# Attention and an MLP on one core: the first batch's value path, the planner's prices and search, and two tiles

## The chip, the cores and the metric

One core of a Trainium2 chip runs the kernel. The time is that of the device in microseconds, the median of several executions; lower is better. The matmul engine is called TensorE (PE in the rows; PEld is its loading of weights), VectorE is DVE, ScalarE is ACT, GpSimd is POOL, and SyncE is SP. SP issues every DMA of this kernel, from one queue, in order.

## The reference

Four batches, 8 heads, 576 positions, head size 64. After the rotation of q and k come softmax attention, a low-rank mixing over the positions, and an MLP with a rectifier; all in float32.

```
q, k = rotate(q), rotate(k)                    # [4, 8, 576, 64]
attn = softmax(q @ k.T / 8)
x    = (attn @ v) as [4, 576, 512]
h    = x.T @ U @ V                             # U [576, 32], V [32, 576]
u    = x + h.T
out  = u + relu(u @ w_ch1) @ w_ch2             # w_ch1 [512, 2048], w_ch2 [2048, 512]
```

U, V and the two weight matrices arrive as 8-byte floats.

## The kernel before

Attention works on pairs of heads (`hp`, four to a batch) and on tiles of 128 query rows (`t`, five to a pair, the last with 64 rows). An ordinary tile has one score tile of 128 x 576 for each of the two heads; the last one holds the 64 rows of both heads in one. That makes nine score tiles a pair. `softmax_tile` takes the row maximum on VectorE (into a scrap tile, `unread`), the exponential on ScalarE, and hands the probabilities to the value matmuls in one of two ways:

- The plain path (`plain_pv`, true for head pairs below `HV` in batch 0; `HV` is 2): five float32 transposes on TensorE by the identity, two copies out of PSUM on ScalarE into a `pt32` tile, and in `values` five float32 matmuls against the values as they are. The sum of the exponentials comes from ScalarE's accumulator.
- The float16 path (all others): ScalarE writes a float16 copy, GpSimd the remainder (`two(p16[:, S:2 * S], p, p16[:, 0:S], ALU.subtract, ...)`), SP issues one DMA transpose of both into a `pt` tile, and `values` runs 14 float16 matmuls against split values (`vh`, `vl`, `vb`). `load_v` makes these from the loaded values: squares on ScalarE for a scale, a high and a low part, and DMA copies. In batch 0 it does so only for the heads from `2 * HV` on, and loads the others straight into `v32`.

`mix` then multiplies by U and V, and `mlp` runs over half batches of 288 positions. The first half of batch 0 is plain as well (`PLH` is 1): float32 matmuls with the weights as `weight` leaves them. `weight` loads 512 KB pieces, 32 in all (16 for each matrix), into staging parts of the tile `wt`, later of `x` and `u`, and `single` turns 8-byte into 4-byte floats with three bit operations a piece on VectorE. When the first half has used them, `convert1` and `convert2` take the squares on ScalarE (scrap output `junk`, which is part of a tile that `unread` uses too), a scale, and then `weight_halves` for each group: ScalarE writes the high float16 half of group g, VectorE or GpSimd the low one. Group g's raw words lie in slot g + 1 of `wt`, so its halves overwrite the raw words of group g - 1. The later half batches run three float16 matmuls for each product, interleaved with the attention of the next batch.

The order on every engine is computed before the kernel is emitted. `Plan` collects each instruction or group as a node with what must come before it; `cost` prices it, `lag` the time between two engines, `place` finds the earliest gap on its engine (a DMA needs a gap on SP's queue, `HW`, and one on the DMA engines), and where several engines can do the work it takes the earliest end. `shares` says which instructions of VectorE and GpSimd exclude each other on a shared port, which is a resource of its own. `schedule` runs a forward pass, then six times a backward pass, whose late times give the next forward pass its order, and keeps the best:

```
best = self.forward(sorted(range(len(key)), key=lambda n: key[n]))
for i in range(6):
    late = self.backward()
    span = self.forward(sorted(late, key=lambda n: (late[n], n)))
    best = min(best, span, key=lambda x: x[0])
```

The nodes are emitted in the order of their planned starts, so every queue runs in this order. All rows carry line 312, where `emit` makes the calls; tiles are told apart by their names.

Of the kernel before, what the change touches and what calls it, by code (L numbers as in the profile page):

```python
# [5 lines left out]

# [5 lines left out]
F32 = mybir.dt.float32  # L12
F32R = mybir.dt.float32r
# [11 lines left out]

PLAIN = HV = 2
GB = 0
# [7 lines left out]
BES = 1  # L35
SKEW = 1

FB = 2


class Plan:
# [86 lines left out]
    def cost(calls):  # L128

        us = 0  # L130
        for eng, op, a, k in calls:
# [5 lines left out]
            if eng == "tensor":  # L137
                m = free(a[1] if op == "transpose" else a[2])
                if op == "transpose":
                    us += free(a[0]) / 1200  # L140
                elif a[2].dtype == F32:

                    k = 2 if list(a[1].ap)[0][1] <= 64 and m > 256 and len(calls) == 4 else 1
                    us += max(m * 4, 640 if free(a[1]) > 1 and m > 1 else 256) / 2400 / k
                    us += 0.05 * (k > 1)
                else:
                    k = 2 if list(a[1].ap)[0][1] <= 64 and len(calls) == 12 else 1
                    us += max(m, 64) * (4 if a[2].dtype == F32R and m < 256 else 1) / 2400 / k
# [9 lines left out]
            elif op == "memset":  # L158
                us += 0.035 + n * 0.00083
            elif op == "tensor_tensor":  # L160
                us += 0.148 + n * (0.0021 if k["in1"].dtype in (F32, F32R) else 0.00189)
            else:
                us += 0.161 + 0.083 * by + n * 0.00083
        return us

# [33 lines left out]

    def place(self, ways, before):  # L200

        found = []
        for calls in ways:
            eng, op, a, k = calls[0]
            ready = max(
                [self.end[j] + self.lag(self.eng[j], eng) for j in before],
                default=0.0,
            )
            if eng == "sync":
                out, in_ = k.get("out", a[0] if a else 0), k.get("in_", a[1] if a else 0)  # L210
                if op == "dma_start_transpose":
                    hw, d = 0.62, 1.01
                else:
                    sb = out if out.space != bass.MemoryType.DRAM else in_
                    rows = list(sb.ap)[0][1]
                    hw, d = 0.45 if rows == 128 else 0.62, rows * free(sb) * SIZE[sb.dtype] / 360e3

                t2 = ready + hw + 0.65
                while True:
                    t2 = self.gap("DMA", t2, d)  # L220
                    t = self.gap("HW", t2 - hw - 0.65, hw)
                    if t <= t2 - hw - 0.65 + 1e-6:
                        break
                    t2 = t + hw + 0.65
                end = t2 + d
                found.append((end, end, t, calls, [("HW", t, hw), ("DMA", t2, d)]))
            else:
                d = self.cost(calls)
                t = self.gap(eng, ready, d)
                held = [eng] + ["port"] * self.shares(calls)  # L230
                while len(held) > 1:
# [10 lines left out]
    @staticmethod  # L242
    def lag(a, b):

        if a == "sync":
            return 0.94
        if a == b:
# [3 lines left out]
    def schedule(self):  # L251
        key = [n[2] for n in self.nodes]
        for n in reversed(range(len(key))):
            for j in self.nodes[n][1]:
                key[j] = min(key[j], (*key[n][:2], j))
        self.key = key
        self.after = [[] for _ in self.nodes]
        for n, (_, before, _) in enumerate(self.nodes):
            for j in before:
                self.after[j].append(n)  # L260
        best = self.forward(sorted(range(len(key)), key=lambda n: key[n]))
        for i in range(6):
            late = self.backward()
            span = self.forward(sorted(late, key=lambda n: (late[n], n)))
            best = min(best, span, key=lambda x: x[0])
        _, self.start, self.end, self.eng, self.chosen, self.busy = best

    def forward(self, order):
# [3 lines left out]
        for n in order:  # L272
            ways, before, _ = self.nodes[n]
            self.end[n], self.start[n], self.chosen[n], held = self.place(ways, before)
            self.eng[n] = self.chosen[n][0][0]
# [5 lines left out]
    def backward(self):  # L281
# [3 lines left out]
        for n in sorted(self.start, key=lambda n: (-self.end[n], -n)):  # L285
            s, e = self.start[n], self.end[n]
            if self.eng[n] == "sync":
                (_, _, hw), (_, _, d) = self.held[n]
                e = s + hw + 0.65 + d
                held = [("HW", e - s - hw, hw), ("DMA", 0.0, d)]  # L290
            else:
                held = [(dev, 0.0, d) for dev, _, d in self.held[n]]
            t = max(
                [done[j] + self.lag(self.eng[n], self.eng[j]) for j in self.after[n]],
                default=0.0,
# [40 lines left out]
def tile_rope_attention_then_mixer(ctx, tc, qk, v, tab, u_in, v_in, w1, w2, out):  # L336
# [83 lines left out]

    wt = cst.tile([P, 2 * NG + 1, 4 * DM], F16, name="wt")
    vst = cst.tile([P, S], F32R, name="vst")
# [184 lines left out]
    def raw_of(g):  # L607
        return wt[:, g + 1, :].bitcast(F32)

# [4 lines left out]

    slot = [pieces(wt[:, s:s + 2, :].rearrange("p s k -> p (s k)")) for s in range(NG + 1, 2 * NG + 1, 2)]
    big = pieces(xs_[1].rearrange("p c s -> p (c s)")[:, NP * S - 4 * DM:] if 1 else xs_[1].rearrange("p c s -> p (c s)")[:, 0:4 * DM])
# [9 lines left out]
    junks = [cst.tile([P, S], BF16, name=f"junk{i}") for i in range(3)]  # L626
    junk = junks[0][:, 0:DM]

# [802 lines left out]
```

## Time and profile before

| | us |
|---|---|
| median of three runs | 686.9 |
| the runs | 682.67, 686.9, 691.01 |
| span of the profiled execution | 684.8 |
| TensorE busy in it | 638.9 |
| VectorE, ScalarE, GpSimd busy | 427.6, 388.4, 232.0 |
| DMA: bytes, share of 16 engines | 86.92 MB, 56% |

The profile is of one execution on the core; its span runs from its first to its last instruction, and its time outside the span was not taken. Busy times of engines overlap. Times in the rows are microseconds from the start of the span unless marked ns. The granted clock of TensorE is 1.00 at 2.4 GHz and 0.50 at 1.2 GHz.

### The profile page before, as it was taken

The numbers are of one execution on the slowest core, as the hardware profiler recorded it, in microseconds if no ns is written. First come the engines' busy times: TensorE is split into PE (matmuls) and PEld (weight loads), VectorE is DVE, ScalarE is ACT, GpSimd is POOL, SyncE is SP. The second block draws the span as 40 slices with busy tenths as digits, with TensorE's granted clock in tenths as the row PEclk, the third lists the DMA queues.
The fourth block names the chain that finished last, engine by engine and source line by source line (L and its number), as shares of the span: only waits on it lengthen the run. The fifth ranks groups of instructions, "written<-read, shape, count | busy, mean of one in ns | idle before, by whom it ended". The sixth has DMA issues, their size and how long they took to land.

```text
span 684.8 us, 15181 instructions
## 1 busy us (share of the span) xinstructions
PE 638.9 (93%) x5952; PEld 486.2 (71%) x5952; DVE 427.6 (62%) x1089; ACT 388.4 (57%) x840; POOL 232.0 (34%) x208
## 2 busy tenths in 40 slices
PE   2899778999898999999999999999999999999997
PEld 1677656677666677777677767777776777777776
DVE  4989687978865765467775875657758652430210
ACT  3756575359887778447765765468566762220210
POOL 1110363113345667154445554264445351000000
PEclk9999899999999999999999999999999999999999
DMA  7799997466464577435768558157664583000000
GB/s 237 243 305 309 246 191 128 155 171 184 93 132 97 123 125 149 92 93 140 158 129 132 119 114 154 64 148 170 118 122 79 88 114 62 18 1 27 10 11 26
DMA packets 178345, 86.92 MB, mean 127 GB/s; under 512 B 152033, under 2 KB 167521, under 8 KB 178273
## 3 DMA queue, kind: packets, MB, share of 16 engines
q1 hardware_dynamic: 178272, 85.96, 56.1%
q8 instruction: 46, 0.75, 0.4%
q14 instruction: 27, 0.21, 0.1%
HBM read 41.70 MB, written 4.72 MB: 68 GB/s over the span
## 4 chain that ended last, share of the span: by engine, by line
PE 57%; DMA 12%; DVE 11%; issue 7%; ACT 6%; POOL 6%; SPq 1%; POOLq 0%; ACTq 0%; DVEq 0%
PE mm L312 42%; PE s L312 10%; DMA pt<-p 9%; PE pv L312 5%; POOL p L312 3%; ACT p L312 3%; DVE wt L312 3%; DVE junk L312 2%; DVE raw L312 2%; DMA raw<-qk 2%; POOL raw L312 2%; DVE qk L312 1%; ACT wt L312 1%; ACT junk L312 1%; SPq L312 1%
## 5 line engine op out<-in xcount | busy, mean ns | idle before, releaser
L312 PEld LDWEIGHTS <-wt 128*128 128x128 f16 x2688 | 256.0, 98 | 73.9 <-issue 12.4
L312 POOL TENSOR_TENSOR p<-p,p 128x576 f16<-128x576 f32 x120 | 158.0, 1328 | 192.8 <-ACT p L312 141.3
L312 PE MATMUL mm<-room,wt 128*128 128x288 f16 (+1 forms) x1472 | 217.9, 298 | 0.0
L312 PE MATMUL mm<-u,wt 128*128 128x288 f16 x1344 | 180.2, 287 | 2.0 <-DVE room L312 2.0
L312 ACT ACTIVATE room<-mm 128x288 f16<-128x288 f32 (+3 forms) x139 | 56.1, 410 | 104.7 <-PE mm L312 104.4
L312 DVE SCALAR_TENSOR_TENSOR room<-mm,room 128x288 f16<-128x288 f32 x112 | 50.8, 456 | 69.1 <-ACT room L312 68.6
L312 PEld LDWEIGHTS <-pt 128*128 128x128 f16 x1722 | 68.4, 98 | 27.3 <-DMA pt<-p 19.7
L312 PE MATMUL s<-qk,qk 64*128 64x288 f16 (+1 forms) x640 | 75.2, 357 | 11.5 <-DVE qk L312 11.2
L312 ACT ACTIVATE p<-p 128x576 f16<-128x576 f32 x120 | 79.3, 681 | 5.2 <-DMA pt<-p 4.0
L312 DVE TENSOR_SCALAR_CACHE_REDUCE junk<-s,bqk 128x576 bf16<-128x576 f32 x72 | 58.0, 811 | 23.0 <-PE s L312 19.6
L312 ACT ACTIVATE p<-s,nb,bqk 128x576 f32<-128x576 f32 x72 | 59.4, 829 | 18.4 <-DVE nb L312 13.2
L312 DVE TENSOR_SCALAR_CACHE_REDUCE junk<-s 128x576 bf16<-128x576 f32 x72 | 52.2, 753 | 27.3 <-PE s L312 24.4
L312 PE MATMUL pv<-vh,pt 128*128 128x65 f16 (+2 forms) x600 | 57.9, 203 | 9.3 <-DMA pt<-p 8.8
L312 ACT ACTIVATE p<-s,nb 128x576 f32<-128x576 f32 x72 | 51.9, 737 | 19.4 <-DVE junk L312 18.2
L312 PE MATMUL pv<-vl,pt 128*128 128x64 f16 (+2 forms) x600 | 57.7, 202 | 0.0
L312 ACT ACTIVATE xf<-pv,rc 128x64 f32<-128x64 f32 (+1 forms) x108 | 29.0, 309 | 43.6 <-DVE rc L312 40.5
L312 PEld LDWEIGHTS s<-qk,qk 64*128 64x128 f32 x256 | 26.0, 203 | 19.4 <-DVE qk L312 11.2
L312 DVE SCALAR_TENSOR_TENSOR ob<-mm,so,x 128x288 f32<-128x288 f32 x28 | 14.4, 513 | 40.5 <-PE mm L312 40.4
L312 DVE TENSOR_SCALAR rs<-pv,sc_v 128x2 f32<-128x2 f32 x63 | 13.7, 218 | 38.8 <-PE pv L312 38.7
L312 PE MATMUL mm<-x,wt 128*128 128x288 f32 x128 | 34.7, 423 | 1.9 <-ACT xf L312 1.1
L312 PE MATMUL pv<-vb,pt 128*128 128x65 f16 (+1 forms) x448 | 33.3, 197 | 0.0
L312 DVE SCALAR_TENSOR_TENSOR wt<-wt 128x512 int32<-128x512 int32 x46 | 31.9, 728 | 0.1
(161 smaller groups left out, 754.9 us busy)
## 6 DMA issues: line engine op xcount, KB each, us to landing
raw<-qk SPq DMA_DIRECT2D x30, 576.0 KB, 4.2
wt<-w SPq DMA_DIRECT2D x23, 512.0 KB, 6.2
out_t<-ob SPq DMA_DIRECT2D x32, 144.0 KB, 1.8
x<-w SPq DMA_DIRECT2D x6, 512.0 KB, 4.5
raw<-vt SPq DMA_DIRECT2D x6, 512.0 KB, 4.2
pt<-p SPq DMA_TRANSPOSE x120, 3.4
vb<-vh SPq DMA_DIRECT2D x6, 264.0 KB, 3.5
u<-w SPq DMA_DIRECT2D x3, 512.0 KB, 4.8
```

The costliest lines, as they stand in the source:

```text
L312: getattr(getattr(nc, eng), op)(*a, **k)
```

## The change

Head pairs 0 and 1 of batch 0 take the float16 path too (`HV` is 0), so the whole first batch does, and `load_v` splits all heads. The raw words of group g move from slot g + 1 to slot g + 2 of `wt` (`RS`), which has one slot more. The scrap tile `junk` gets memory of its own (`SQJ`). The planner's prices change: DMA transposes cost 1.37 us on SP's queue and 1.3 us on the DMA engines (0.62 and 1.01 before), other DMAs signal later, and several matmul groups cost 0.05 to 0.3 us more. `schedule` first does what it did, then applies 52 moves one after the other: each adds seeded random shifts to the late times in one stretch, plans three times, and is kept if the planned end is earlier. The memory set aside for DMA descriptors made by GpSimd becomes 1024 bytes a partition.

```
-PLAIN = HV = 2
+PLAIN = HV = 0
...
+RS = 2
+MOVES = (
+    (2201, 0.3, -489, 100), (7090, 0.3, -200, 40), (3748, 0.3, -65, 10), (365, 0.3, -230, 10),
...
+)
+SQJ = 1
...
                 if op == "transpose":
                     us += free(a[0]) / 1200
+                    if "xf" in a[1].tensor.name:
+                        us += 0.05 if free(a[0]) > 64 else 0.12
...
+        if eng == "tensor" and op == "matmul":
+            if list(a[1].ap)[0][1] <= 64 and len(calls) in (4, 12):
+                us += 0.18 if len(calls) == 12 else 0.06
+            elif len(calls) == 5 and free(a[2]) == 256:
+                us += 0.3
+            elif a[2].dtype == F32R:
+                us += 0.07
+            elif free(a[2]) <= 2:
+                us += 0.12
...
+    @staticmethod
+    def transfer(calls):
+
+        _, op, a, k = calls[0]
+        out, in_ = k.get("out", a[0] if a else 0), k.get("in_", a[1] if a else 0)
+        if op == "dma_start_transpose":
+            return 1.37, 0.9, 1.3, 0.98
+        sb = out if out.space != bass.MemoryType.DRAM else in_
+        rows = list(sb.ap)[0][1]
+        hw = 0.45 if rows == 128 else 0.62
+        return hw, hw + 0.65, rows * free(sb) * SIZE[sb.dtype] / 360e3, 1.2
...
         if a == "sync":
-            return 0.94
+            return 0.98 if turn else 1.2
...
+        best = self.settle(sorted(range(len(key)), key=lambda n: key[n]), 7)
+        for seed, width, begin, wide in MOVES:
+            best = min(best, self.shaken(best, seed, width, begin, wide), key=lambda x: x[0])
...
+    def shaken(self, best, seed, width, begin, wide):
+
+        draw = Random(seed)
+        late = {
+            n: t + draw.gauss(0, width) if begin <= t < begin + wide else t
+            for n, t in sorted(best[-1].items())
+        }
+        for n in reversed(range(len(late))):
+            for j in self.nodes[n][1]:
+                late[j] = min(late[j], late[n])
+        return self.settle(sorted(late, key=lambda n: (late[n], n)), 3)
...
-    wt = cst.tile([P, 2 * NG + 1, 4 * DM], F16, name="wt")
+    wt = cst.tile([P, 2 * NG + RS, 4 * DM], F16, name="wt")
...
-        return wt[:, g + 1, :].bitcast(F32)
+        return wt[:, g + RS, :].bitcast(F32)
...
-    junk = junks[0][:, 0:DM]
+    junk = cst.tile([P, DM], BF16, name="junk") if SQJ else junks[0][:, 0:DM]
...
-    nc = bacc.Bacc("TRN2", target_bir_lowering=False, num_devices=1)
+    nc = bacc.Bacc(
+        "TRN2", target_bir_lowering=False, num_devices=1,
+        dynamic_dma_scratch_size=1024,
+    )
```

## Rows read from the trace of the kernel before

**Rows 1.** the page: busy time by engine; shares of the chain that ended last

```profile
...
PE 638.9 (93%) x5952; PEld 486.2 (71%) x5952; DVE 427.6 (62%) x1089; ACT 388.4 (57%) x840; POOL 232.0 (34%) x208
...
PE 57%; DMA 12%; DVE 11%; issue 7%; ACT 6%; POOL 6%; SPq 1%; POOLq 0%; ACTq 0%; DVEq 0%
...
```

**Rows 2.** stages: busy us (x instructions) by engine, granted clock, DMA share, GB/s

```profile
...
0.00:13.00 13.00, 1.75 (x8) 1.18 (x8) 5.43 (x15) 4.36 (x7) 1.66 (x12) 1.00 0.71 220
13.00:74.00 61.00, 56.32 (x372) 44.37 (x368) 55.73 (x137) 39.73 (x116) 6.82 (x10) 0.97 0.89 288
43.00:69.00 26.00, 25.32 (x180) 20.25 (x181) 25.35 (x63) 17.06 (x50) 0.79 (x1) 1.00 0.92 311
74.00:124.50 50.50, 38.66 (x374) 27.24 (x373) 38.03 (x96) 28.52 (x59) 23.95 (x21) 0.90 0.90 164
78.00:80.00 2.00, 0.06 (x2) 0.06 (x3) 0.59 (x1) 1.51 (x3) 0.99 (x1) 0.50 0.84 191
124.50:580.00 455.50, 441.38 (x4387) 333.77 (x4388) 302.59 (x785) 299.85 (x622) 199.53 (x166) 1.00 0.60 124
240.00:253.00 13.00, 12.13 (x140) 8.94 (x138) 9.67 (x26) 11.13 (x23) 8.83 (x9) 1.00 0.84 136
...
```

**Rows 3.** timeline of TensorE, 40 to 75, the plain path

```profile
...
42.52 1.37 PE L312 MATMUL pv<-vh,pt 128*128 128x64 f32 x10
...
45.21 0.98 PE L312 MATMUL mm<-ident,p 128*128 128x128 f32 x7
...
51.61 0.77 PE L312 MATMUL mm<-ident,p 128*128 128x128 f32 x5
...
72.20 0.43 PE L312 MATMUL pv<-vh,pt 128*128 128x64 f32 x2
...
74.40 0.27 PE L312 MATMUL pv<-vl,pt 64*128 64x64 f32 x1
...
```

**Rows 4.** timeline of TensorE, 226 to 235, the float16 path

```profile
...
226.19 0.23 PE L312 MATMUL pv<-vh,pt 128*128 128x130 f16 x1 [0.41 <-DMA pt<-p]
...
227.00 1.51 PE L312 MATMUL mm<-u,wt 128*128 128x288 f16 x11
...
233.25 0.19 PE L312 MATMUL pv<-vh,pt 128*128 128x65 f16 x1
...
234.09 0.29 PE L312 MATMUL mm<-u,wt 128*128 128x288 f16 x1
...
```

**Rows 5.** groups of instructions with shapes, whole run

```profile
...
L312 POOL TENSOR_TENSOR p<-p,p 128x576 f16<-128x576 f32 x120 | 158.0, 1328 | 192.8 <-ACT p L312 141.3 <-issue 48.0 <-POOL p L312 2.0
L312 ACT ACTIVATE p<-p 128x576 f16<-128x576 f32 x120 | 79.3, 681 | 5.2 <-DMA pt<-p 4.0
...
L312 ACT ACTIVATE pt<-mm 128x512 f32<-128x512 f32 x12 | 7.0, 590 | 1.7 <-PE mm L312 1.7
...
```

**Rows 6.** DMA transposes on SP's queue, 239 to 253: duration ns min/median/max

```profile
...
L312 SPq DMA_TRANSPOSE pt<-p x7: 1260/1298/2087, 239.8 to 251.8; - x7
...
```

**Rows 7.** groups of VectorE with shapes, 0 to 124.5

```profile
...
L312 DVE SCALAR_TENSOR_TENSOR wt<-wt 128x512 int32<-128x512 int32 x42 | 29.3, 733 | 0.1
...
L312 DVE TENSOR_SCALAR wt<-wt 128x512 int32<-128x512 int32 x23 | 9.3, 422 | 0.0
...
L312 DVE SCALAR_TENSOR_TENSOR vl<-raw,sc_v,vh 128x256 f16<-128x256 f32 x3 | 1.5, 519 | 0.0
...
```

**Rows 8.** loads of weights on SP's queue, 0 to 124.5, into the tile wt

```profile
...
L312 SPq DMA_DIRECT2D wt<-w x23: 368/375/630, 19.7 to 96.2; - x23
...
```

**Rows 9.** timeline, 107 to 114: GpSimd beside VectorE

```profile
...
108.76 3.81 POOL L312 TENSOR_TENSOR p<-p,p 128x576 f16<-128x576 f32 x3 [1.88 <-ACT p L312]
...
111.45 1.67 DVE L312 SCALAR_TENSOR_TENSOR wt<-wt 128x512 int32<-128x512 int32 x1
...
```

**Rows 10.** timeline of ScalarE, 165 to 200: the weights' conversion

```profile
...
179.59 1.15 ACT L312 ACTIVATE wt<-wt,sck_a 128x1024 f16<-128x1024 f32 x1 [1.03 <-DVE wt L312]
...
```

**Rows 11.** what TensorE waited for, whole run

```profile
...
PE pv L312 <- DMA pt<-p: 8.8, 12, 2.2
...
```

More of the change, by code (lines that the diff above doesn't have):

```diff
@@ L5 @@
 from itertools import cycle
+from random import Random
 import concourse.bass as bass
@@ L198, in take, with place @@
             b.insert(i, [t, t + d])
-    def place(self, ways, before):
+    @staticmethod
[8 more added lines that the diff above has]
+        return hw, hw + 0.65, rows * free(sb) * SIZE[sb.dtype] / 360e3, 1.2
+    def place(self, n):
+        _, before, _ = self.nodes[n]
         found = []
-        for calls in ways:
-            eng, op, a, k = calls[0]
+        for calls, eng, d, port in self.ways[n]:
             ready = max(
-                [self.end[j] + self.lag(self.eng[j], eng) for j in before],
+                [self.end[j] + self.lags[self.eng[j], eng, j in self.turns] for j in before],
                 default=0.0,
@@ L255, in schedule, with settle @@
                 key[j] = min(key[j], (*key[n][:2], j))
-        self.key = key
         self.after = [[] for _ in self.nodes]
-        for n, (_, before, _) in enumerate(self.nodes):
+        self.turns = set()
+        self.ways = []
+        for n, (ways, before, _) in enumerate(self.nodes):
             for j in before:
                 self.after[j].append(n)
-        best = self.forward(sorted(range(len(key)), key=lambda n: key[n]))
-        for i in range(6):
-            late = self.backward()
-            span = self.forward(sorted(late, key=lambda n: (late[n], n)))
-            best = min(best, span, key=lambda x: x[0])
-        _, self.start, self.end, self.eng, self.chosen, self.busy = best
+            if ways[0][0][1] == "dma_start_transpose":
+                self.turns.add(n)
+            self.ways.append([
+                (c, c[0][0], self.transfer(c) if c[0][0] == "sync" else self.cost(c), self.shares(c))
+                for c in ways
+            ])
+        names = ("tensor", "vector", "scalar", "gpsimd", "sync")
+        self.lags = {
+            (a, b, t): self.lag(a, b, t) for a in names for b in names for t in (False, True)
+        }
+        best = self.settle(sorted(range(len(key)), key=lambda n: key[n]), 7)
+        for seed, width, begin, wide in MOVES:
+            best = min(best, self.shaken(best, seed, width, begin, wide), key=lambda x: x[0])
+        _, self.start, self.end, self.eng, self.chosen, self.busy, _ = best
+    def settle(self, order, turns):
+        best = None
+        for _ in range(turns):
+            found = self.forward(order)
+            late = self.backward()
+            if best is None or found[0] < best[0]:
+                best = (*found, late)
+            order = sorted(late, key=lambda n: (late[n], n))
+        return best
+    def shaken(self, best, seed, width, begin, wide):
[3 more added lines that the diff above has]
+            for n, t in sorted(best[-1].items())
+        }
+        for n in reversed(range(len(late))):
+            for j in self.nodes[n][1]:
+                late[j] = min(late[j], late[n])
+        return self.settle(sorted(late, key=lambda n: (late[n], n)), 3)
     def forward(self, order):
@@ L272, in forward @@
         for n in order:
-            ways, before, _ = self.nodes[n]
-            self.end[n], self.start[n], self.chosen[n], held = self.place(ways, before)
+            self.end[n], self.start[n], self.chosen[n], held = self.place(n)
             self.eng[n] = self.chosen[n][0][0]
@@ L292, in backward @@
                 held = [(dev, 0.0, d) for dev, _, d in self.held[n]]
+            turn = n in self.turns
             t = max(
-                [done[j] + self.lag(self.eng[n], self.eng[j]) for j in self.after[n]],
+                [done[j] + self.lags[self.eng[n], self.eng[j], turn] for j in self.after[n]],
                 default=0.0,
@@ L613, in pieces @@
         return [t[:, h] for h in range(2)]
-    slot = [pieces(wt[:, s:s + 2, :].rearrange("p s k -> p (s k)")) for s in range(NG + 1, 2 * NG + 1, 2)]
+    slot = [pieces(wt[:, s:s + 2, :].rearrange("p s k -> p (s k)")) for s in range(NG + RS, 2 * NG + RS, 2)]
     big = pieces(xs_[1].rearrange("p c s -> p (c s)")[:, NP * S - 4 * DM:] if 1 else xs_[1].rearrange("p c s -> p (c s)")[:, 0:4 * DM])
```

26 lines of the change are left out of this document (10 added, 16 removed), and 13 rows, old and new, of the table MOVES.

## The prediction

> **What bounds the kernel now.** I read the busy table first, then the chain that ended last, then busy time by stage, then what TensorE waited for. TensorE is busy 638.9 us of the 684.8 us span, and the chain is mostly its matmuls [rows 1]. So an edit is worth what it takes off TensorE's work, plus the idle time it removes, less the idle time it adds. Idle time there is 684.8 - 638.9 = 45.9 us, and the stages [rows 2] say where: 11.25 us before 13.0 (the first score matmul waits for loads and rotation), 61.0 - 56.3 = 4.7 us up to 74.0 (head pairs 0 and 1 of batch 0, the path that is replaced), 50.5 - 38.7 = 11.8 us up to 124.5 (head pairs 2 and 3 in the float16 path, then the mixing), 14.1 us in all the 455.5 us up to 580, and about 4 at the end. After 124.5 the kernel is a saturated TensorE with little to gain; before it, it is not. In that first stretch two other things run nearly full: VectorE, 25.35 of the 26 us from 43 to 69, and the DMA engines, at 0.89 and 0.90 of their time. Whatever comes off TensorE in the first stretch is paid out only as far as these two let the first MLP start earlier than 124.5.
>
> **The change, first part: TensorE's work.** In the plain path of head pairs 0 and 1 each score tile costs five float32 transposes and five float32 value matmuls (ten records). Two neighbouring tiles run from 42.52 to 45.21, so 1.35 us each; five transposes take up to 0.77 us, about 0.7 us to the next instruction; the tile of the last 64 rows, which serves both heads, has twenty value records from 72.20 to about 74.6, 2.4 us [rows 3]. In the float16 path two tiles take 233.25 to 234.09, so 0.42 us each, and the last-rows tile 226.19 to 227.00, 0.81 us; the transposes are gone from TensorE [rows 4]. There are 2 x 8 ordinary and 2 x 1 last tiles: 16 x (1.35 + 0.70 - 0.42) + 2 x (2.4 + 0.70 - 0.81) = 26.1 + 4.6 = **30.7 us off TensorE**, all before 74.
>
> **Second part: what takes its place.** Each of the 18 tiles gains one ScalarE conversion (0.68 us) and loses the evacuation of its transposes (0.59 us for the wide one alone), so ScalarE stays as it is or gains; it is busy 39.7 of 61 us there, with room. Each gains a GpSimd subtraction of 1.33 us, 18 x 1.33 = 23.9 us on an engine that now idles there [rows 2, 5]. Each gains a DMA transpose. Seven of them were issued between 239.8 and 251.8, each holding SP's queue 1.30 us (median) [rows 6], while the DMA engines were busy 0.84 of 240 to 253 [rows 2]: 0.84 x 13 / 7 = 1.56 us of the 16 engines each, which is an upper bound as other packets ran too. 18 x 1.56 = 28 us more DMA time in a stretch that is at 0.9 already. The split of the values doubles in width (head pairs 0 and 1 skip it now); on VectorE I take 2.5 us, the low parts of a quarter being 0.52 us [rows 7], and zero on TensorE's path, as it ends before the first values are due if the order puts it first; if it is late, the first values wait a few us.
>
> **When can the first MLP start?** I make four sums for the point that is now 124.5, each from its rows, leaving out what need not be done by then. That is chiefly the second weight matrix: 16 of the 32 pieces of weights belong to the first one, and by 124.5 at least 23 were issued, those to the tile wt alone, the last at 96.2 [rows 8], and 42 of the 64 long bit operations were done [rows 7].
> TensorE: 124.5 - 30.7 = **94**.
> VectorE: 5.4 + 55.7 + 38.0 = 99.2 us busy [rows 2], less 10 x 0.73 and 7 x 0.42 = 10.3 us of the second matrix [rows 7], plus 2.5 for the values, is 91.4; with its 7.6 us idle up to 13, it can't be done before **99**, and at the density of 13 to 74 (0.91) it is **107**.
> DMA: 0.71 x 13 + 0.89 x 61 + 0.90 x 50.5 = 109 us; a piece of weights is 0.52 MB, at 311 GB/s and 0.92 share (43 to 69) 1.55 us, so seven of them less is -11; the loads of batch 1 that could wait are estimated at -8; plus 28: **118**, or some 12 less if the last two groups of the first matrix (four pieces, 6 us) land beside the MLP and a transpose costs 1.2 us rather than its upper bound.
> The SBUF port that VectorE and GpSimd share: three subtractions ran back to back from 108.76 to 112.57, and a bit operation of VectorE that took 0.73 us on average was recorded from 111.45 for 1.67 us, ending when it could run after them [rows 9]. If they exclude each other, GpSimd's 32.4 us up to 124.5 [rows 2], less an estimated 2 for memsets, plus 23.9, and the VectorE operations that the planner's `shares` counts to the port (32 x 0.73 + 16 x 0.42 for the first matrix and an estimated 24 for rotation and small parts) make 54 + 54 = 108 us from about 7: **115**, less up to 8 if the last two groups of the first matrix are converted while the MLP has begun.
> On this the Trainium skill's page "SBUF — State Buffer", section "Who interferes with whom", is stricter than I am: a GpSimd operation and such a VectorE operation never overlap, the later one blocks for the whole of the other. The row agrees with it for one case. By it the sum would be 115 and nothing earlier without shifting conversions.
> So TensorE is no longer what decides the first stretch: three bounds lie between 99 and 118. I take **110, a gain of 14.5 us**, toward the upper end, because the port and DMA sums are the tightest and order on three in-order engines is never perfect; ends 99 (25 us) and 124.5 (0).
>
> **Third part: the conversion of the weights.** With one slot between a group's raw words and its halves, the next group's halves wait until VectorE has read the last raw words: ScalarE's conversion at 179.59 waited 1.03 us for VectorE [rows 10]. With two slots it need not. TensorE was still busy nearly all that time, so of the 14.1 us idle from 124.5 to 580 this is worth between 0 and 3; I take 2. The scrap tile removes a false order between ScalarE's squares and VectorE's maxima; both have room: 0 to 1 us, taken as nothing, covered by TensorE's matmuls. The DMA scratch size touches no transfer here, since all are issued from SP: nothing.
>
> **Fourth part: the order.** Every instruction's place is recomputed with longer prices (a DMA transpose holds its queue 1.37 us instead of 0.62; the trace's median is 1.30 [rows 6]) and improved by 52 random perturbations, each kept only if the planned end is earlier. That can't change the amount of work, only idle time. The value matmuls into the tile pv alone waited 8.8 us in twelve places for transposes to land [rows 11], a thing that was priced too low. The 16.5 us idle from 13 to 124.5 are already in the sums above. Of the 14.1 behind that, less the 2 of part three, I take a third, 4 us; ends -2 (a tight plan meets other durations and slips) and 9. What is moved past what: SP's queue is in order, 18 more transposes hold it 18 x 1.3 = 24 us and each waits there for its GpSimd subtraction; weights queued behind them come later by that wait, and VectorE's conversions behind those.
>
> **Sum.** 684.8 - 14.5 - 2 - 4 = 664.3 us of span; TensorE then is busy about 608 us and idle 56: 16 us more than now before the MLP, 6 less behind its start. The median of the three runs, 686.9, stands 2.1 above the profiled span, so the forecast is **666.5 us**.
>
> **Rivals.** (a) TensorE's saving is paid out in full: conversions and loads of the first matrix spread into the MLP, start at 99 or earlier, and the order takes 7 more: 684.8 - 25 - 9 + 2 = **653**. For it: 30.7 us of TensorE work really go, and VectorE has a third of its time free after 124.5. Against: three resources above. (b) The first stretch stays as long as it is: DMA and port at their upper sums, plus waits, put the MLP's start at 120 to 124.5, and of parts three and four only half, 3 us, remains: 684.8 less 0 to 4.5, less 3, plus 2.1, or **679 to 684**. For it: head pairs 2 and 3 in this very path and the mixing took 50.5 us with few weights to load and the DMA engines at 0.90, and TensorE's granted clock was 0.50 in 78 to 80 while it idled [rows 2], so idle time comes back as slow matmuls. Against: the same stretch has VectorE at 38 of 50.5 us. (c) Slower: the transposes stand ahead of weights on SP. If the 18 x 1.56 us of DMA and the 24 us of SP's queue delay the last pieces of the first matrix one for one, its conversion ends at 124.5 + 28 - 11 = 141 at the worst, and at 135, half way from the upper sums, the total is 684.8 + 10.5 - 4 + 2 = **693**. It decides as soon as the last first-matrix piece is issued after about 115; before, the last of all pieces to wt was issued at 96.2 [rows 8]. The Trainium skill's page "VectorE: DVE Perf Modes", section "The three transpose paths", gives 390 ns for a 128 x 128 transpose on TensorE and 1309 ns by DMA, and its rules prefer TensorE where PSUM will do. By that rule this change goes the wrong way, to (c); the rows say that the two aren't exchanged one for one, since TensorE is the engine that is full and a transfer of nine blocks costs it nothing.
>
> **How the numbers follow.** Measured runs of this kernel spread by 0.6%, so 1% (6.9 us) is about what counts. Forecast 0.57 (its own range 655 to 678); (a) 0.16; (b) 0.16; (c) 0.11. The range of 8 in 10, **650 to 687**, holds the forecast, most of (a) and most of (b), and leaves (c) out. Faster than 680: forecast, (a) and a third of (b), 0.78; within 1%: the rest of (b), 0.11, and 0.02 of (c), 0.13; slower: 0.09.
>
> **What would show it.** Right: TensorE busy 605 to 612 us; the 90 float32 transposes and 200 float32 value records gone; first f32 MLP matmuls in a run at 105 to 114; more TensorE idle time before that point than 28 us; idle from there to the last 100 us below 12 us. Wrong: the MLP's start at 120 or later (b), the last piece of the first weight matrix issued after 115 (c), or a start below 100 (a). If TensorE's busy time does not fall by 25 us or more, the first sum is wrong; low granted clock in the first stretch would be the reason to look for.

## The result, and the profile after

In the first comparison the changed kernel takes 676.9 us (673.07 to 678.41, four executions) against 684.8 for the one before on the same chip: a ratio of 0.988, 95% interval 0.984 to 0.992. A second comparison (e1 below) gives 677.85 and 0.988; the ten executions together have a median of 677.6. The kernel is faster by 1.2%, 8 us; 666.5 was forecast, a gain of 20. The time lies in the range, the sign is right, and the size is off by a factor of more than two.

The profiled execution of the changed kernel took 673.07 us, the fastest of its four, its span 671.3, so 1.8 us lie outside the span. Its page, answering to [rows 1]:

```profile
PE 620.9 (92%) x5914; PEld 467.9 (70%) x5914; DVE 437.1 (65%) x1096; ACT 388.1 (58%) x794; POOL 239.1 (36%) x205
...
PE 50%; DMA 7%; DVE 3%; issue 2%; ACT 2%; POOL 2%; SPq 0%; ACTq 0%; POOLq 0%; DVEq 0%
```

TensorE's busy time fell by 18.0 us; 30.7 were to go. The stages, with the columns of [rows 2] (the third row lies inside the second), cut where the mixing of batch 0 ends. I take the first matmul into mm from squ for that point (it makes a scale that only the later half batches need): 125.8 in the kernel before, 120.6 here. By the prediction's own point, the last start of MLP matmuls ahead of it, 124.5 became 118.7.

```profile
0.00:13.00 13.00, 1.84 (x8) 1.19 (x8) 5.58 (x16) 3.81 (x4) 1.81 (x11) 1.00 0.75 241
13.00:74.00 61.00, 43.80 (x362) 28.63 (x362) 46.68 (x110) 38.11 (x73) 31.72 (x24) 0.86 1.02 221
43.00:69.00 26.00, 21.48 (x204) 14.46 (x205) 20.59 (x49) 17.89 (x35) 16.44 (x13) 0.76 1.02 226
74.00:120.60 46.60, 37.30 (x351) 26.28 (x352) 39.20 (x98) 32.37 (x78) 22.77 (x18) 0.93 1.05 256
120.60:566.30 445.70, 436.46 (x4379) 331.67 (x4377) 319.02 (x815) 297.63 (x604) 182.76 (x152) 1.00 0.65 140
```

From 13 to 74 TensorE does 12.5 us less, and the granted clock falls from 0.97 to 0.86. VectorE, nearly full before, has air (20.6 of 26 us instead of 25.35). GpSimd gained 24.9 us, as costed (23.9). The DMA engines' share, 0.89 and 0.90, became 1.02 and 1.05. The share adds up the time of packets and can pass 1 (1.25 in one stretch of 8 us of e1 below), so the rows alone don't show that the engines are at their limit; e6, e9 and e12 bear on that. TensorE does its smaller work, slower, and then waits.

The profile of e1, the same kernel in another execution (680.25 us, the slowest of its six), shows how much of this is steady. Its stages, columns as above:

```profile
13.00:74.00 61.00, 41.70 (x357) 28.11 (x356) 45.74 (x110) 39.11 (x76) 32.30 (x25) 0.85 1.03 218
74.00:126.00 52.00, 42.03 (x357) 29.86 (x355) 40.32 (x99) 31.64 (x75) 22.90 (x18) 0.83 0.97 236
```

And its transposes into pt on SP's queue, 13 to 126 (how long each holds the queue, in ns, then the time to landing):

```profile
L379 SPq DMA_TRANSPOSE pt<-p x22: 1242/1364/3170, 17.0 to 110.0; - x22
...
DMA to landing us min/median/max: 3.2/4.1/7.0
```

Here the mixing ends at 126.0, and the MLP matmuls ahead of it start at 123.4: the same program, some 5 us apart. So the first stretch (to the end of the mixing) changed by -5.2 us in one execution and +0.2 in the other, where -14.5 was forecast. Behind it, to the span's end, 559.0 us became 550.7 and 552.5: -8.3 and -6.5, where -6 was forecast. **The larger part of the gain lies behind the first stretch** (8.3 of 13.5 us in one execution, all of it in the other), although TensorE was relieved inside it. There, most of it lies in the first two half batches of the MLP: 172.9 us together before, 166.8 and 168.4 after. A single half says less, since attention of the next batch runs among them and can move from one to the other.

### The profile page after: what moved, and what is told of

The parts are those of the page before. It is cut to its first block, busy times and chain, and to the rows that moved or that the text cites. A ratio compares the mean times of both kernels' runs of the same rounds, so it can differ in the third digit from the quotient of the medians.

```text
span 671.3 us, 15150 instructions
## 1 busy us (share of the span) xinstructions
PE 620.9 (92%) x5914; PEld 467.9 (70%) x5914; DVE 437.1 (65%) x1096; ACT 388.1 (58%) x794; POOL 239.1 (36%) x205
## 4 chain that ended last, share of the span: by engine, by line
PE 50%; DMA 7%; DVE 3%; issue 2%; ACT 2%; POOL 2%; SPq 0%; ACTq 0%; POOLq 0%; DVEq 0%
PE mm L379 38%; PE s L379 7%; DMA pt<-p 5%; PE pv L379 5%; DMA raw<-qk 1%; ACT p L379 1%; POOL p L379 1%; DVE junk L379 1%; DVE room L379 0%; DVE raw L379 0%; DVE u L379 0%; POOL raw L379 0%; ACT room L379 0%; SPq L379 0%; DVE x L379 0%
## 5 line engine op out<-in xcount | busy, mean ns | idle before, releaser
L379 POOL TENSOR_TENSOR p<-p,p 128x576 f16<-128x576 f32 x130 | 171.6, 1328 | 209.3 <-ACT p L379 144.7
L379 PE MATMUL mm<-u,wt 128*128 128x288 f16 x1344 | 183.6, 286 | 1.7 <-DVE room L379 1.4
L379 ACT ACTIVATE room<-mm 128x288 f16<-128x288 f32 (+1 forms) x128 | 52.0, 408 | 97.1 <-PE mm L379 90.1
L379 PE MATMUL s<-qk,qk 64*128 64x288 f16 (+1 forms) x640 | 84.7, 371 | 18.8 <-DVE qk L379 11.2
L379 PEld LDWEIGHTS <-pt 128*128 128x128 f16 x1918 | 79.0, 100 | 29.6 <-DMA pt<-p 16.6
L379 ACT ACTIVATE p<-p 128x576 f16<-128x576 f32 x130 | 86.9, 681 | 12.1 <-DMA pt<-p 10.6
L379 PE MATMUL pv<-vh,pt 128*128 128x65 f16 (+1 forms) x600 | 57.4, 200 | 6.7 <-DMA pt<-p 5.6
L379 PE MATMUL pv<-vl,pt 128*128 128x64 f16 (+1 forms) x600 | 57.2, 200 | 0.3 <-DVE vl L379 0.3
L379 PEld LDWEIGHTS s<-qk,qk 64*128 64x128 f32 x256 | 30.2, 216 | 33.0 <-ACT p L379 13.0
L379 DVE TENSOR_SCALAR rs<-pv,sc_v 128x2 f32<-128x2 f32 x67 | 14.5, 217 | 29.8 <-PE pv L379 28.5
L379 ACT ACTIVATE x<-mm 128x128 f32<-128x128 f32 (+1 forms) x59 | 15.5, 263 | 30.7 <-PE mm L379 30.5
```

The lines of the kernel that those rows point to most:

```text
L379: getattr(getattr(nc, eng), op)(*a, **k)
```

## The experiments

Medians are compared with 677.6 for the changed kernel, 684.8 to 686 for the one before. "Mixing" is the end of the mixing, "second half" the second half batch of the MLP (90.6 us in the changed kernel, 90.4 before), from the addition that ends one half to the next such addition.

**The parts by themselves.** e1 repeats the changed kernel, with no edit.

> The changed kernel once more, beside the others of this group, to size the gain and to tell how far single profiled spans can be trusted. From the first comparison (0.988): 0.984 to 0.992 of the kernel before, and a first MLP stretch that begins at 117 to 120, as in its profile (118.7).

677.85 us, 0.988 [0.983, 0.993]. The result stands; the start of the MLP does not: 123.4, outside the 117 to 120 expected.

e2 is the kernel before with the path alone; old prices, one slot, no search:

```
-PLAIN = HV = 2
+PLAIN = HV = 0
```

> The kernel before with only HV = 0: the float16 path for the whole first batch, old prices, no search, one slot, shared scrap. Theory A (the 30.7 us taken off TensorE are swallowed by the first stretch itself, because there each tile's chain of scores, maximum and exponential or the DMA engines set the pace, not TensorE): 0.995 to 1.01, MLP begins at 118 to 126. Theory B (the path does pay, and the new order gives its gain away): 0.97 to 0.985, MLP at 105 to 112.

700.8 us, 1.0245 [1.020, 1.029]: **slower by 2.4%**, beyond both theories. Mixing at 127.2, about as before; the second half takes 107.6 us instead of 90.4. There its TensorE is busy 35.8 of 45 us at 0.84 of the clock (the stage 210 to 255):

```profile
210.00:255.00 45.00, 35.82 (x337) 25.99 (x337) 30.71 (x85) 35.53 (x73) 28.86 (x22) 0.84 0.58 118
```

and ScalarE's conversion of the weights, just before, waits for VectorE (its timeline, 180 to 210):

```profile
186.87 1.15 ACT L312 ACTIVATE wt<-wt,sck_a 128x1024 f16<-128x1024 f32 x1 [1.47 <-DVE wt L312]
...
203.22 1.15 ACT L312 ACTIVATE wt<-wt,sck_a 128x1024 f16<-128x1024 f32 x1 [1.05 <-DVE wt L312]
```

The kernel before has waits of the same length (1.03 us in [rows 10]), so they alone don't explain the loss. It converts earlier; the eight conversions of the first matrix, before and in e2:

```profile
L312 ACT ACTIVATE wt<-wt,sck_a x8: 1148/1148/1150, 169.3 to 190.6; 128x1024 f16<-128x1024 f32 x8
```

```profile
L312 ACT ACTIVATE wt<-wt,sck_a x8: 1147/1148/1165, 182.7 to 203.2; 128x1024 f16<-128x1024 f32 x8
```

From 210 to 255 TensorE of e2 waits 4.9 us for ScalarE's output xf, 0.3 in the kernel before. In the changed kernel's timeline three such conversions run on end, in 3.63 us:

```profile
181.29 3.63 ACT L379 ACTIVATE wt<-wt,sck_a 128x1024 f16<-128x1024 f32 x3
```

and its stage 210 to 255 has TensorE busy 43.65 us at full clock:

```profile
210.00:255.00 45.00, 43.65 (x447) 32.17 (x445) 35.57 (x91) 35.17 (x71) 28.73 (x23) 1.00 0.61 134
```

e3 is all but the path, e4 all but the search, e14 the changed kernel with its 52 moves drawn from other seeds (still each kept only if the plan gets shorter):

```
e3:  +PLAIN = HV = 2
e4:  +MOVES = ()
e14: the first number of each of the 52 moves + 10000
```

> The changed kernel with HV = 2 again: plain path for head pairs 0 and 1, but the new prices, the search, two slots and the own scrap tile. Theory A: the gain is mostly the order's, so 0.985 to 0.993 with the MLP beginning at 122 to 126 and less idle TensorE behind it. Theory B: without the path nothing is gained, 0.995 to 1.005.

690.35 us, 1.008 [1.0045, 1.012]; mixing at 128.6. Slower than either theory had it.

> The changed kernel with an empty list of moves: float16 path, new prices, two slots, own scrap, and the seven passes as before. If the search carries the gain behind the MLP's start: 0.993 to 1.003, idle time of TensorE after 124 back at 13 us or more. If the prices carry it: 0.986 to 0.991, the same as with the search.

692.75 us, 1.010 [1.006, 1.015], slower than both cases had it.

> The changed kernel with every seed of the 52 moves raised by 10000: the same stretches, widths and count, other random shifts, none of which was picked beforehand. If the gain needs those seeds (they are the few of thousands that shortened the plan): 1.00 to 1.012 of the kernel before, close to the kernel without search (1.010). If any search of this size does: 0.985 to 0.993.

681.7 us, 0.9945 [0.991, 0.998]; mixing at 127.3; between the two cases. So without search the whole change is slower than the kernel before; 52 moves that nobody picked bring 11 us, picking the seeds another 4. The nearest thing to a price of the path compares two plans with unpicked moves: e3 to e14, 690.35 to 681.7, **-8.7 us**, of which the first stretch holds 1.3. The two first stretches, without the path and with it:

```profile
0.00:128.60 128.60, 103.55 (x752) 77.59 (x752) 100.79 (x247) 84.60 (x218) 38.38 (x42) 0.91 0.82 230
```

```profile
0.00:127.30 127.30, 84.33 (x714) 58.28 (x715) 93.25 (x225) 74.84 (x154) 57.97 (x52) 0.85 0.99 231
```

The path takes 19.2 us off TensorE's busy time here, and 17.9 of them come back as idle time. At the end of the second half batch the two profiles still stand level (295.4 and 295.9); the whole difference arises behind it, where both kernels have the same work. With one draw of moves on either side it is therefore not shown that the 8.7 us are the path's and not the draw's.

**The slot and the scrap tile.** The picked moves fit one plan only, so e14 is the base here. Each of the three runs below is again one plan.

```
e8:  +RS = 1
     +SQJ = 0
e15: +SQJ = 0
e16: +RS = 1
```

> The changed kernel with RS = 1 and SQJ = 0: one slot between raw words and halves, the scrap tile shared again, order planned anew with the same seeds. My sum gave the slot 2 us and the scrap nothing: 1 to 4 us slower than the changed kernel. Rival: they carry most of what was gained behind the MLP's start, 6 to 8 us slower.

693.8 us, 1.013 [1.008, 1.018]; second half 99.7 (92.6 in e14), TensorE busy 37.05 of the 45 us from 210 at 0.89.

> The changed kernel with the scrap tile shared again (SQJ = 0), two slots kept, order planned anew with the same seeds, which were picked for the whole change. My sum has the scrap at nothing: within 4 us of the changed kernel with other seeds (681.7). Rival: the false order between squares and maxima is what the run without slot and scrap lost (693.8): 688 or more.

683.5 us, 0.999 [0.996, 1.002], as my sum had it.

> The changed kernel with one slot again (RS = 1), own scrap tile kept, planned anew with the same seeds. If the slot carries the 10 us that the half batch after the plain one lost with one slot: 688 to 694 and that half batch back at 98 us or more. If the two together are needed: 682 to 686.

684.05 us, 0.997 [0.994, 1.000], as expected if the two together are needed. Undoing either costs about 2 us, which is inside the intervals, undoing both 12, beyond what either case of e8 had; some 7 of the 12 lie in the second half, where e2 has its loss. My reading, not shown: the weights' conversion must be done beside attention there, the path pushes it later, and with one of the two tiles the order can still keep conversion and squares apart, with neither it can't.

**What sets the first stretch.** Four suspects: the half clock, the DMA engines, the port that GpSimd and VectorE share, VectorE itself. e5 keeps TensorE busy with two float32 matmuls into an unused part of a PSUM bank ahead of each group of scores:

```
+for _ in range(2):
+    nc.tensor.matmul(spare, ones, cs[:, 0, 0:256], start=True, stop=True)
```

> The changed kernel, same order, with two extra float32 matmuls (256 columns of constants into an unused part of a PSUM bank, result not used) ahead of each group of scores of batch 0 but the first, so that TensorE does not idle there. They cost some 40 x 0.43 = 17 us of TensorE at full clock. Theory C (the first stretch is slow since TensorE idles, its granted clock falls to 1.2 GHz, and the scores on the tile's chain then take 2.3 to 3.6 us instead of 1.24): granted clock from 13 to 74 rises from 0.86 to 0.97 or more, MLP begins 3 to 8 us earlier than 118.7, 0.988 to 0.995 of the changed kernel. Rival (DMA or GpSimd set the pace): same or up to 5 us later.

682.7 us, 0.9955 [0.992, 0.999]. Its stages:

```profile
48.00:98.00 50.00, 42.34 (x448) 30.14 (x446) 36.68 (x92) 33.55 (x70) 30.73 (x25) 0.98 1.06 205
98.00:129.00 31.00, 23.14 (x186) 16.36 (x187) 24.26 (x59) 16.13 (x44) 9.58 (x8) 0.83 0.91 242
```

and its score matmuls among TensorE's groups up to 130 (count, busy us, mean ns, idle before them):

```profile
L385 PE MATMUL s<-qk,qk 64*128 64x288 f32 x128 | 28.7, 531 | 16.4 <-DVE qk L385 11.5 <-ACT p L385 4.9
```

The clock came back in the middle only: 0.98 from 48 to 98, where the changed kernel has 0.88 (0.82 in e1). From 13 to 74 it is 0.86, as without fillers, so the sign that theory C asked for was not produced. The scores take 28.7 us instead of 34.5, and the mixing ends at 129.4. The fillers cost 23.9 us of TensorE, far more than the 5.8 that the scores give back, so the run shows that these fillers do not pay; what the slow clock costs it does not show.

e6 issues eight loads of the first matrix a second time, e9 leaves eight of its sixteen out:

```
e6: +    nc.sync.dma_start(self.spare.pop(0), a[1])
e9: +    if n in self.left_out: continue
```

> The changed kernel, same order, with eight of the 512 KB weight loads of the first matrix issued twice (second copy to memory that nothing reads), between 50 and 110. Theory D (the DMA engines, at 1.02 to 1.13 of their time there, set the first stretch): each costs its 1.55 us, so the MLP begins 9 to 13 us later, at 128 to 131, and the time rises as much. Theory C or the tile's chain: later by 0 to 4 us, the time within 0.6%.

686.35 us, 1.004 [1.001, 1.007]: 1.1 us for each load more; mixing at 132.5. That is theory D's way, at less than its price; each load more also holds SP's queue (0.46 us or more), so queue and engines are not told apart.

> The changed kernel, same order, with eight of the sixteen 512 KB loads of the first weight matrix left out (the words that the other eight brought are converted again, so half of that matrix is wrong). Theory D (the DMA engines set the first stretch): 8 x 0.8 to 1.55 us back, so the mixing of batch 0 ends 6 to 12 us earlier than in the changed kernel's second profile (126.0), the time 4 to 12 us lower. Rival theories: 0 to 2 us.

678.2 us, 0.988 [0.984, 0.993]; mixing at 126.0. Theory D is not met. The DMA share fell only from 95 on (0.70 up to 115; 0.94 in e1), and the mixing ends where it did in e1: in the last quarter of the stretch the DMA engines did not set the pace. For the time before, this run tells nothing.

e10 to e13 shorten the work of one suspect each, and of all three:

```
e10: +k = {i: x[:, 0:144] ...}   # GpSimd's subtractions of batch 0 behind the fifth, 576 columns before
e11: +k = {i: x[:, 0:128] ...}   # VectorE's second and third bit operations of the first matrix, 512 before
e12: +k = dict(out=k["out"][:, 0:4], in_=k["in_"][:, 0:512])  # transposes behind the fifth, 1152 before
e13: all three
```

> The changed kernel, same order, with 31 of the 36 GpSimd subtractions of batch 0 cut to a quarter of their columns (the low halves of the probabilities stay old in the rest). It takes some 31 x 0.95 = 29 us off GpSimd and off the port that it shares with VectorE, and 0.95 us off each tile's way from exponential to transpose. Theory P (port or GpSimd set the pace): end of the mixing 8 to 20 us earlier. Theory D: 0 to 3 us.

674.3 us, 0.983 [0.9785, 0.987]; mixing at 122.1, between the two executions of the uncut kernel (120.6 and 126.0). Theory P is not met.

> The changed kernel, same order, with the second and third bit operation on each piece of the first weight matrix cut to a quarter of its columns (that matrix is wrong then). It takes 32 x some 0.5 = 16 us off VectorE and off the port in the first stretch. Theory V (VectorE sets the pace): end of the mixing 8 to 16 us earlier; theory P: 3 to 8; theory D: 0 to 3.

676.25 us, 0.985 [0.980, 0.990]; mixing at 121.5. No change that stands out of the spread.

> The changed kernel, same order, with 31 of the 36 DMA transposes of batch 0 cut from nine blocks to four (the rest of each transposed tile keeps old words). It takes up to 31 x 0.87 = 27 us off the DMA engines and shortens each transfer's way. Theory D, in the form that the transposes and not the weights are what the DMA engines choke on: end of the mixing 6 to 14 us earlier than in the second profile (126.0). If the pace is set elsewhere: 0 to 3 us.

670.1 us, 0.979 [0.9755, 0.982]; mixing at 115.3, earlier than in both executions, as theory D has it.

> The changed kernel, same order, with the cuts of three runs at once: short subtractions, short bit operations, short DMA transposes in batch 0. If one of the three sets the pace and the next is close behind it, the whole is more than the sum of the single cuts: 10 us or more under the changed kernel. If the pace is that of the order itself (each tile waits its turn on in-order engines, whatever the resource costs), it is no more than their sum, 5 to 8 us.

664.0 us, 0.970 [0.967, 0.973]; mixing at 111.0. Against 677.6 the cuts give 3.4, 1.4 and 7.5 us, 12.3 in sum and 13.6 together: about their sum, and the transposes are more than half (the 1.4 of e11 lie inside the interval). With only the transposes short (e12), the stages are:

```profile
13.00:74.00 61.00, 44.90 (x376) 30.27 (x374) 47.07 (x115) 40.04 (x79) 34.17 (x26) 0.86 0.86 196
74.00:115.00 41.00, 30.80 (x335) 22.31 (x334) 38.18 (x92) 29.54 (x71) 20.91 (x17) 1.00 0.74 201
```

the transposes on SP's queue:

```profile
L384 SPq DMA_TRANSPOSE pt<-p x22: 1188/1196/2758, 16.9 to 100.1; - x22
...
DMA to landing us min/median/max: 2.4/3.4/6.8
```

and what TensorE waited for, 13 to 115.3 (us, times, longest):

```profile
PE s L384 <- ACT p L384: 8.6, 9, 4.3
PE mm L384 <- DVE x L384: 4.6, 5, 1.4
```

In the changed kernel the last of these views has, 13 to 120.6,

```profile
PE s L379 <- ACT p L379: 8.9, 9, 4.3
PE mm L379 <- DMA pt<-p: 4.2, 5, 1.8
PE mm L379 <- DVE x L379: 3.6, 5, 1.4
```

The wait for pt goes with the cut, the DMA share from 1.05 to 0.74. The longest waits, of scores for ScalarE's exponentials, stay, and with them the clock of 0.86 up to 74. Behind 74 the clock is 1.00 (0.93 in the changed kernel, 0.83 in e1). From 13 to the end of the mixing, changed kernel and e12:

```profile
13.00:120.60 107.60, 81.10 (x711) 54.91 (x710) 85.88 (x207) 70.48 (x150) 54.49 (x42) 0.89 1.03 236
```

```profile
13.00:115.30 102.30, 76.00 (x711) 52.79 (x710) 85.55 (x207) 69.75 (x150) 55.08 (x42) 0.92 0.81 199
```

The same 711 records, the same idle time of TensorE (26.5 and 26.3 us): against this execution the 5.3 us are nearly all busy time of TensorE, at a higher mean clock. Against e1 (83.7 busy, 29.3 idle) it is both. Whether short transposes help by their DMA time, by their shorter way or through the clock that follows is not separated. Taken together, e6 and e12 speak for the DMA engines or SP's queue as what sets most of the first stretch, e9 speaks against them in its last quarter, and no run shows a single cause for the whole.

**The planner.** e7 lets three score tiles be under way at once (`S3 = 1`), which could fill those waits:

> The changed kernel with S3 = 1: a third score tile for batch 0, made of the two PSUM banks that the value and mixing matmuls of batch 0 shared with it (the values keep one bank), order planned anew with the same seeds. If the two score tiles set the pace (a score group waits until the exponential has emptied its tile): TensorE's wait of scores for the exponential (8.9 us before 124) falls below 4 and the MLP begins 3 to 8 us earlier. If not, or if the lost banks weigh as much: 0 to 6 us later.

677.4 us, 0.988 [0.983, 0.992]; mixing at 124.4; the wait is 6.6 us, not below 4. Nothing gained.

e17 puts one of the two head pairs on the path, with moves picked for it; e18 tells the planner what the trace shows of its DMAs, with moves picked for that:

```
e17: -PLAIN = HV = 0
     +PLAIN = HV = 1                      # and 93 moves
e18: -    return 1.37, 0.9, 1.3, 0.98     # a DMA transpose
     +    return 1.37, 1.2, 1.6, 0.98
     -    ... / 360e3, 1.2                # other DMAs
     +    ... / 330e3, 1.2                # and 101 moves
```

> The changed kernel with only head pair 1 of batch 0 added to the float16 path (HV = 1, head pair 0 stays plain), and a list of 93 moves picked for this case by a search of the same kind, to a planned end of 642.5 us (645.1 in the changed kernel). If the DMA transposes set the first stretch's pace, nine of them less let the mixing end at 116 to 121 and the time is 671 to 676. If what the path takes off TensorE is what pays, half of it is given away: the mixing ends at 123 or later and the time is 679 to 683 in spite of the better planned end.

676.7 us, 0.985 [0.9795, 0.990]. Neither theory's pair of numbers: the mixing ends at 127.4, later than in the changed kernel, and the second half takes 82.7 us instead of 90.6, which pays for it. With half of the path the total is the same; a plan with as many picked moves and the path in no head pair was not run.

> The changed kernel with the planner's DMA prices set to what the trace of the changed kernel shows: a transpose is priced 1.6 us of the DMA engines (1.3) and 1.2 us more to its landing (0.9), other transfers 330 GB/s (360); and a list of 101 moves picked for these prices by a search of the same kind, to a planned end of 647.0 us in these prices. If wrong DMA prices are why the plan slips in the first stretch, the mixing ends at 112 to 118 and the time is 668 to 674. If the slip comes from durations that no price holds (the half clock, one execution against another), the mixing ends at 120 to 126 and the time is 676 to 681.

674.8 us, 0.985 [0.980, 0.990], between the two theories. The transposes land in 3.5 us (median) instead of 4.1, but the mixing's own matmuls come no sooner: its product s from vst starts at 119.9, at 115.1 and 119.7 in the two executions of the changed kernel. Planned 647.0, measured 27.8 us more; the changed kernel's plan of 645.1 misses by 32.5. So better DMA prices, with a longer search, closed some 5 of these 32 us. That e18 is better than the changed kernel by 0.4% lies inside both intervals and is not settled.

## Why the prediction was right and wrong

**The step that failed** is the choice between the four sums: "So TensorE is no longer what decides the first stretch: three bounds lie between 99 and 118. I take 110, a gain of 14.5 us". That TensorE would not decide was right. But 110 lies below two of the four sums, and each of them assumes that its engine never waits, while a transposed tile passes ScalarE, GpSimd, SP's queue and the DMA engines one after the other. Measured, the MLP's start is 118.7 and 123.4 (the end of the mixing 120.6 and 126.0), at or above the largest sum (118, DMA):

```profile
0.00:118.70 118.70, 81.11 (x710) 54.93 (x710) 89.62 (x219) 73.39 (x151) 56.30 (x53) 0.90 1.00 235
```

So the gain of this part was 5.8 and 1.1 us instead of 14.5. The DMA sum itself came close: a mean share of 1.00 over 118.7 us. TensorE did not idle more than the forecast has it: 37.6 us up to here, where 110 - (96.7 - 30.7) = 44 follow from it. It was busy 81.1 us instead of 66. e13 gives the scale: only with most transposes at 44%, and most subtractions and two of three bit operations of the first matrix at 25% of their columns, does the MLP start at 109.1 and the mixing end at 111.0, where I had put the start at 110 with all of them whole. What happened is nearest to rival (b), by its mechanism (DMA and port at their upper sums, plus waits; it had the start at 120 to 124.5), at a time 2 us below its range.

**TensorE's work: the count right, the time not.** The float32 transposes and value matmuls are gone, but busy time fell by 18.0, not 30.7. TensorE's groups up to 126 show where most of the other 12.7 went, first before, then after:

```profile
L312 PE MATMUL s<-qk,qk 64*128 64x288 f32 x128 | 24.7, 484 | 11.2 <-DVE qk L312 11.2
```

```profile
L379 PE MATMUL s<-qk,qk 64*128 64x288 f32 x128 | 34.5, 573 | 18.8 <-DVE qk L379 11.2 <-ACT p L379 7.5
```

The same 128 records of score matmuls take 9.8 us more, at a granted clock of 0.86 where the kernel before had 0.97 (13 to 74). The prediction named a low clock as what to look for, but priced it at nothing. What it costs in time is not settled: e5 did not remove it, and e12 gained with the clock unchanged up to 74 and at 1.00 behind.

**GpSimd, ScalarE, SP: right.** GpSimd gained 24.9 us (23.9), ScalarE lost 1.6 up to 74 ("stays as it is or gains"), a transpose holds SP 1.36 us (1.30). What I had not priced was the landing: 4.1 us (median) from issue in e1, 3.4 before, with the DMA engines full; five waits of TensorE for it before the mixing, 4.2 us.

**The port.** The sum of port work, part of it estimated, put the MLP's start at 115 if the two engines never overlap. With the port's work whole and short transposes (e12) it is 113.4 and the mixing ends at 115.3; with the port's work cut too (e13) the mixing ends at 111.0. By the Trainium skill's page "SBUF — State Buffer", section "Who interferes with whom", the shared port is an exclusive lock; these times are about what that gives, without proving it. With the subtractions alone cut (e10) the mixing ended at 122.1 and the time fell by only 3.4 us: the port looks like the next bound, not the first.

**Slot and scrap tile: mis-sized.** I took 2 us for the slot and nothing for the scrap tile, "covered by TensorE's matmuls". Each alone is worth about 2 (e15, e16), both 12 (e8), each from one plan. The cover was read from the kernel before; with the path alone (e2) its conversions come 13 us later. I costed one part against the old schedule of the other.

**The order: right size, in part by luck.** Behind the first stretch -6 was forecast and -6.5 to -8.3 measured; TensorE's idle time there fell from 18.1 to 12.8 and 14.2 us. But it isn't idle time polished away from a given plan: without moves the change loses (e4), and with prices, tiles and unpicked moves but without the path it also loses (e3, 690.35). Between e3 and e14 the first half batch is shorter by 7.7 us and the second longer by 9.5, since work moves from one to the other (555 and 805 records of TensorE in e3, 435 and 928 in e14); what is left of the 8.7 us comes from the third (2.7) and the sixth (3.4). That the sizes agree with the forecast is no sign that its reason was right.

**Rival (c)** stood nearer than its time says: the last piece of the first matrix was issued at about 111 in the profiled execution, but at 115.6 in e1, past the 115 from which it was to decide; leaving those late pieces out gained nothing (e9), and the change is not slower. The Trainium skill's page "VectorE: DVE Perf Modes", section "Rules for kernel authors", would keep the transposes on TensorE. The path alone did lose 2.4% (e2), the sign of that rule; but the loss sits in the second half batch, not in the first stretch, and slot, scrap tile and search together turned it round.

**Left open:** why the plan slips by about 28 us even with the traced DMA prices; whether the path, with a search of equal length on both sides, beats one head pair less (e17) or none; and how far plans of equal search differ by their draw alone.

## What to carry to other kernels

When work moves from a full engine to several others, take the largest of the resource sums as the floor and not as the pessimist's end: here a chain through four in-order queues ended at or above it, so add the waits along one item's chain before choosing a value, and price the relieved engine's slower work. A buffer that costs nothing in the present schedule must be priced in the schedule that the rest of the change makes; undo parts together as well as singly. And a searched order hides the price of what it orders: compare two versions only with equal search on both, and with more than one draw.

## What the runs showed of the hardware

The half clock in one place: in the changed kernel eight records of float32 score matmuls took 3.63 us in a stretch with a granted clock of 0.50 (1.2 GHz) and 1.89 us at 1.00 (2.4 GHz), ten microseconds later:

```profile
44.74 3.63 PE L379 MATMUL s<-qk,qk 64*128 64x288 f32 x8 [0.15 <-ACT p L379]
...
54.31 1.89 PE L379 MATMUL s<-qk,qk 64*128 64x288 f32 x8 [0.49 <-ACT p L379]
```

From 38 to 50 TensorE was busy 9.68 of 12 us in its records, at a mean clock of 0.61: low clock makes an engine look busy that has little to do.

The port, from e1: the timeline, 33 to 39, shows two of VectorE's rotation steps beside two subtractions of GpSimd:

```profile
33.55 4.06 POOL L379 TENSOR_TENSOR p<-p,p 128x576 f16<-128x576 f32 x2 [2.09 <-ACT p L379]
34.43 2.05 DVE L379 TENSOR_TENSOR raw<-raw,csq 128x1152 f32<-128x1152 f32 x1 [0.30 <-DMA raw<-qk]
36.51 1.71 DVE L379 TENSOR_TENSOR qk<-raw 128x576 f32<-128x576 f32 x1
```

Of the same two steps over the whole run, the view by tile has min, median and max in ns:

```profile
L379 DVE TENSOR_TENSOR raw<-raw,csq x16: 751/1354/2439, 8.6 to 502.2; 128x1152 f32<-128x1152 f32 x14, 128x576 f32<-128x576 f32 x2
...
L379 DVE TENSOR_TENSOR qk<-raw x10: 748/757/1712, 7.9 to 208.9; 128x576 f32<-128x576 f32 x10
```

So 2.05 us stand against a median of 1.35, 1.71 against 0.76, and the two subtractions' 4.06 against 2 x 1.33: VectorE took 1.65 us longer and GpSimd 1.40. And one program differed by 5.4 us in its first stretch between two executions (120.6, 126.0) while the rest agreed within 1.8: with the DMA engines full, an in-order schedule may carry each late landing on; that is a reading, not shown.
